# First MLP layer of two token blocks by Strassen-Winograd products, with folded weights kept in memory

## The chip, the core and the metric

The kernel runs on one core of a Trainium2 chip. A core has a matrix engine (TensorE, PE in the profile, with weight loads listed apart as PEld), a vector engine (DVE), a scalar engine (ACT), GpSimd (POOL), and SyncE (SP), which here only issues DMA transfers. Each engine works through its own queue of instructions in program order; semaphores tie the queues together. SBUF is the memory on the chip, with 128 partitions; PSUM is the memory that PE adds into, eight banks of 128x512 fp32. The metric is the device time of one execution in microseconds (us).

## The reference

x holds 2048 tokens of 640 features. xn is its layer norm. The output is x plus a linear attention of xn plus an MLP of xn with its own layer norm.

```python
xn = _layernorm(x, axis=-1)
return x + _A_ref(xn, A_wqkv, A_w_phi, A_wo) + _B_ref(xn, B_w1, B_b1, B_w2, B_b2)
...
qkv = (xn @ wqkv) -> q, k, v                          # 32 heads of 20
phi_q = [softmax(q @ w_phi), softmax(-q @ w_phi)]     # phi_k likewise
o = phi_q (phi_k^T v) / (phi_q phi_k^T 1), then @ wo
...
y = _layernorm(xn)
h = _gelu(y @ w1 + b1)                                # 640 -> 1728
return h @ w2 + b2                                    # 1728 -> 640
```

## The kernel before

**Arithmetic.** Every matmul of weight is done on fp32 operands that are split into a high and a low fp32r part. `split` (lines 50 to 60) does it: ACT copies the high part, and DVE or POOL subtracts it from the source for the low one. `mm3` (62 to 65) then runs three matmuls into the same bank, high by high, high by low and low by high; lines 63, 64 and 65 in the profile are these three. A product of 128 x 128 weights with 128 x 512 tokens is thus three matmuls of 128x512.

**Stages.** The 2048 tokens are four blocks of 512. Stage 1, up to about 225 us, runs the MLP of blocks 0 and 1 and, beside it, makes ready what the attention needs. Then come the projections to q, k and v (`proj`, for 16 tiles of 128 tokens and four banks of columns, which end at `CB` = 456, 908, 1362, 1856), the features and the k-v sums; then the MLP of blocks 2 and 3 beside the attention; then the output projection.

**The MLP in stage 1.** The 1728 hidden values are 14 chunks of 128; the last has 64. The five K chunks of 128 features make 15 matmuls for a chunk (`first`, line 242), after which `gelu` (249) has ACT read the bank, copy the high part, and DVE make the low part. Chunk 13 takes its high and low columns side by side, 10 matmuls, then an add on DVE and a subtraction on POOL (L278). A group g is two chunks. `passes(g, b, ws)` (253 to 295) is a generator: its first `next` runs the first layer of group g for block b, the rest the second layer, five output tiles m of 6 matmuls each (5 for the last group), each of which DVE adds into `acc[b]` (L293 with the bias for g = 0, L295 for the others). The second layer of one pass is run behind the first layer of the next. PSUM banks 0 to 2 (`ph`) are for the first layer, 3 and 4 (`px`) for work beside it, 5 to 7 (`po`) for the second layer: three outputs can stand before the first must be added.

**The work beside.** After every few matmuls the MLP steps a generator, `mlp.beside`. In most of stage 1 that is `prep` (478 to 531): it folds w_phi into the weights of k and q (L456, eight small matmuls and a split for the first part of each of 12 groups), takes statistics of blocks 2 and 3, splits the weights of v, transposes the statistics and sends them through memory (`rows`, 179, once for each block), and makes the normalised y of these blocks (L518, L521, L525, L528), stored to `y_dram`. The folded weights of k, v and the first of q stay in SBUF in `wkv_`; the other q weights go to `wq_dram` and are loaded at L573 for the projections.

**What sets the order.** PE's order is the program's throughout (`manual_schedule`, line 302). From line 351 to 558 (`order`) DVE, ACT and POOL keep the program's order too. A scheduler places the DMA issues on SP. After stage 1, L560 stores `acc` of the two blocks.

Of the kernel before, what the change touches and what calls it, by code (L numbers as in the profile page):

```python
# [15 lines left out]
P = 128  # L16
# [28 lines left out]
def tile_kernel(ctx: ExitStack, tc: tile.TileContext, x, xT, wkT, wqT, wv, wphi, wo, w1, b1, w2, b2,  # L45
# [24 lines left out]
    ones1 = cp.tile([1, P], F32, name="ones1")  # L70
# [11 lines left out]
    wq_dram = [tc.dram_tile([P, KC, CB[3] - CB[2]], F32, name=f"wq{p}") for p in "hl"]  # L82
    wo_dram = [tc.dram_tile([P, KC, D], F32, name=f"wo{p}") for p in "hl"]
    o_dram = [tc.dram_tile([2 * DH, 512], F32, name=f"o{b}") for b in range(NB)]
    r_dram = [tc.dram_tile([8, P], F32, name=f"r{b}") for b in range(NB)]
# [93 lines left out]
    def rows(b, xp, ptile):  # L179

        sc = xp.tile([P, 2, 4], F32, name="sc", bufs=1)
        nc.vector.tensor_copy(sc[:, 0, :], mv[:, 4 * b:4 * b + 4, 0])
        nc.vector.tensor_copy(sc[:, 1, :], ry[:, 4 * b:4 * b + 4])
        for _ in range(2):
            yield
        ps = ptile()
        nc.tensor.transpose(ps[:8, :P], sc.rearrange("p a t -> p (a t)"), idt)
        sr = xp.tile([8, P], F32, name="sr8", bufs=1)
        nc.vector.tensor_copy(sr, ps[:8, :P])
        nc.sync.dma_start(r_dram[b], sr)  # L190
        mr = mtile(5)
        nc.sync.dma_start(mr.rearrange("p a t -> p (a t)"),
                          r_dram[b].rearrange("r t -> (r t)").unsqueeze(0).to_broadcast([P, 8 * P]))
        return mr


    class Mlp:
        def __init__(self, slots, hid):
            self.hid, self.turn, self.slots, self.beside, self.raw = hid, 0, slots, iter(()), {}
            self.ph, self.px, self.po = Banks(0, 1, 2), Banks(3, 4), Banks(5, 6, 7)  # L200
# [14 lines left out]
        def take(self, c):  # L215
            w, parts = self.take_parts(c)
            for p in parts:
                p()
            return w

        def take_parts(self, c):

            r1, r2 = self.raw.pop(c)
            w = wp.tile([P, 4, D], F32R, name=f"w{self.slots[c % 4]}")
# [3 lines left out]
            def last():  # L228


                split(w1h[:, :, 0:64], w1h[:, :, 64:128], r1[:, :, 0:64])
                nc.vector.memset(f(w1l[:, :, 64:128]), 0.0)
                nc.vector.tensor_copy(w1l[:, :, 0:64], f(w1h[:, :, 0:64]))
                nc.scalar.activation(w2h, r2, AF.Copy)
                nc.vector.memset(f(w2l[64:128, :]), 0.0)
                nc.vector.tensor_tensor(w2l[0:64, :], r2[0:64, :], f(w2h[0:64, :]), op=ALU.subtract)

            return (w1h, w1l, w2h, w2l), [last] if c == 13 else [
# [14 lines left out]
        def passes(self, g, b, ws, hid=None):  # L253
# [7 lines left out]
            for j, (w1h, w1l, w2h, w2l) in enumerate(todo):  # L261
# [6 lines left out]
                else:  # L268
                    pz = self.ph()
                    for kc in range(KC):  # L270
                        nc.tensor.matmul(pz, w1h[:, kc, :], yh[:, kc, :], start=kc == 0, stop=False)
                        nc.tensor.matmul(pz, w1l[:, kc, :], yl[:, kc, :], start=False, stop=kc == KC - 1)
                    tm = gt[0:64, :]
# [6 lines left out]
            yield  # L280
            for m in range(KC):
# [12 lines left out]
                else:  # L294
                    nc.vector.tensor_tensor(acc[b][:, m, :], pw, acc[b][:, m, :], op=ALU.add)  # L295

# [42 lines left out]
    for c, pool in ((2, None), (3, r0)):  # L339
# [5 lines left out]
    for c in range(2, 4):  # L345
        dmas[c][1]()
    load_acc(0)
    for c in range(4):
        wc[c], parts[c] = mlp.take_parts(c)
# [33 lines left out]
    parts[2][0]()  # L383
# [5 lines left out]
    parts[3][0]()  # L389
# [26 lines left out]
    p10 = mlp.passes(1, 0, [wc[2], wc[3]])  # L416
    next(p10)
    finish(p00)
    for c in range(2, 4):
        parts[c][1]()  # L420
# [5 lines left out]
    mlp.fetch(4)  # L426

    wkv = ExitStack()
    kvw = wkv.enter_context(tc.tile_pool(name="wkv", bufs=1, side="right", reuse_waits="tile"))

    wkv_ = [kvw.tile([P, KC, CB[2]], F32R, name=f"wk{p}") for p in "hl"]
    rs = ExitStack()
    fp = rs.enter_context(tc.tile_pool(name="prep", bufs=2, side="right", reuse_waits="tile"))
    wpt = fp.tile([G6, 6, 6, DH], F32, name="wpt", bufs=1)
    nc.sync.dma_start(wpt, wphi)

    def raws(n, g):
        kk = G6 if g < 5 else 2 * DH
        raw = fp.tile([P, D], F32, name="raw")
        nc.sync.dma_start(raw[:kk, :], {"k": wkT, "q": wqT}[n][g * G6:g * G6 + kk, :])  # L440
        return raw

    def prep_fold(n, g, raw):
# [3 lines left out]
        if n == "k" or g == 0:  # L447
            c = slice(g * G5, g * G5 + kd) if n == "k" else slice(QK + D, CB[2])
            dst = [w[:, :, c] for w in wkv_]
        else:  # L450
            t = fp.tile([P, 2, KC, G5], F32R, name="t")[:, :, :, :kd]
            dst = [t[:, p] for p in range(2)]
        for k, ni in ((0, 4), (4, 1)):
# [4 lines left out]
            split(dst[0][:, k:k + ni], dst[1][:, k:k + ni], ps[:, :ni * kd].rearrange("p (i f) -> p i f", i=ni))  # L458
            for _ in range(3):
                yield  # L460
        if n == "q" and g:
            for p in range(2):
                nc.sync.dma_start(wq_dram[p][:, :, (g - 1) * G5:(g - 1) * G5 + kd], f(t[:, p]))

    def more_stats():

        for b in range(2, 4):
            def tiles():
                xbs = {}
                for t in (*range(4 * b, 4 * b + 4), None):  # L470
                    if t is not None:
                        xbs[t] = fp.tile([P, 2, KC, G5], F32, name="t").rearrange("p a c f -> p (a c f)")[:, :D]
                        nc.sync.dma_start(xbs[t], x[t * P:(t + 1) * P, :])
                    if xbs and t != 4 * b:
                        yield xbs.pop(min(xbs))
            yield from stats(range(4 * b, 4 * b + 4), fp, tiles())

    def prep():
        jobs = [(n, g) for n in "kq" for g in range(6)]
# [631 lines left out]
```

## Time and profile before

| | us |
|---|---|
| time, three runs | 737.65, 738.07, 739.62 (median 738.07) |
| profiled execution, span | 736.8 |
| first folding matmuls (L456) | 52.9 |
| first projection | 225.4 |

The profiled execution's own time is not given apart from its span; the median of the runs is 1.3 us above the span, which is what lies around it. In a row of the timeline stand the start, the duration, the engine, line, operation and its output and inputs, and in brackets how long the engine was idle before and what ended that. In a row of groups stand the count, the busy time, the mean in ns, and the idle time before.

### The profile page before, as it was taken

What the parts mean: (1) busy time and instruction counts of PE and PEld (TensorE: products, weight loads), DVE (VectorE), ACT (ScalarE), POOL (GpSimd) and SP (SyncE); (2) the same over time, 40 slices, a digit from 0 to 9 for tenths busy, and PEclk for the clock granted to TensorE, in tenths of its full rate; (3) what the DMA queues carried; (4) which work ended last, traced back from release to release, by engine and by line L of the source; (5) the groups of instructions that cost most, each with busy time, mean ns of one, the idle gap of its engine ahead of it and who ended that gap; (6) DMA issues with size and microseconds to landing.
All of it is one profiled execution on the core that took longest, in us unless ns stands there. A gap on an engine that the chain in (4) does not pass through costs nothing.

```text
span 736.8 us, 9681 instructions
## 1 busy us (share of the span) xinstructions
PE 723.8 (98%) x3441; PEld 610.2 (83%) x3441; DVE 479.9 (65%) x790; ACT 320.5 (44%) x526; POOL 370.6 (50%) x322
## 2 busy tenths in 40 slices
PE   9999999998999999999999999999999999999998
PEld 7788888777788998998998888888878888877886
DVE  7847645665653788788888788645575656767331
ACT  6624444332322464464345357256565556440110
POOL 2211222343321797797778889445586777304000
PEclk9999999999999999999999999999999999999999
DMA  9704477464543223633600706853433353153222
GB/s 317 221 19 141 143 177 178 141 193 142 159 161 144 75 86 144 161 101 150 143 0 1 179 1 200 196 149 107 126 116 114 113 157 90 48 215 127 83 84 73
DMA packets 64520, 95.36 MB, mean 129 GB/s; under 512 B 13312, under 2 KB 35216, under 8 KB 62848
## 3 DMA queue, kind: packets, MB, share of 16 engines
q1 hardware_dynamic: 64184, 94.74, 42.5%
q8 instruction: 27, 0.44, 0.3%
q14 instruction: 21, 0.17, 0.1%
q10 hardware_dynamic: 288, 0.01, 0.0%
HBM read 64.47 MB, written 30.26 MB: 129 GB/s over the span
## 4 chain that ended last, share of the span: by engine, by line
PE 73%; DVE 10%; DMA 5%; POOL 5%; ACT 3%; issue 3%; SPq 0%; POOLq 0%; DVEq 0%; ACTq 0%
PE bank L63 22%; PE bank L65 21%; PE bank L64 21%; PE bank L659 2%; PE bank L456 2%; POOL m L628 2%; PE bank L882 1%; DMA m<-r 1%; PE bank L881 1%; DVE acc L295 1%; DVE y L946 1%; DVE rx L925 1%; DVE m L57 1%; DMA raw<-in_wv 1%; DMA xb<-in_x 1%
## 5 line engine op out<-in xcount | busy, mean ns | idle before, releaser
L57 POOL TENSOR_TENSOR w<-r,w 128x640 fp32r<-128x640 f32 x52 | 83.2, 1618 | 107.6 <-ACT w L54 77.4
L63 PE MATMUL bank<-y,w 128*128 128x512 f32 (+1 forms) x334 | 131.1, 392 | 0.9 <-ACT m L250 0.6
L65 PE MATMUL bank<-y,w 128*128 128x512 f32 (+1 forms) x334 | 129.8, 389 | 0.3 <-POOL w L57 0.3
L64 PE MATMUL bank<-y,w 128*128 128x512 f32 (+1 forms) x334 | 129.6, 388 | 0.0
L63 PE MATMUL bank<-m,w 128*128 128x512 f32 x260 | 104.3, 401 | 4.6 <-DVE acc L295 3.8
L65 PE MATMUL bank<-m,w 128*128 128x512 f32 x260 | 101.8, 392 | 0.0
L64 PE MATMUL bank<-m,w 128*128 128x512 f32 x260 | 101.7, 391 | 0.0
L295 DVE TENSOR_TENSOR acc<-bank,acc 128x512 f32<-128x512 f32 x120 | 80.7, 682 | 16.7 <-PE bank L65 11.1
L57 DVE TENSOR_TENSOR m<-m,m 128x512 fp32r<-128x512 f32 (+1 forms) x54 | 45.0, 834 | 67.1 <-ACT m L54 67.1
L63 PE MATMUL bank<-wkh,y 128*128 128x456 f32 (+2 forms) x240 | 88.6, 369 | 0.0
L64 PE MATMUL bank<-wkl,y 128*128 128x456 f32 (+2 forms) x240 | 88.5, 369 | 0.0
L65 PE MATMUL bank<-wkh,y 128*128 128x456 f32 (+2 forms) x240 | 88.4, 368 | 0.0
L63 PEld LDWEIGHTS bank<-y,w 128*128 128x128 f32 x334 | 62.8, 188 | 14.1 <-DVE ob L1050 0.8
L65 PEld LDWEIGHTS bank<-y,w 128*128 128x128 f32 x334 | 62.7, 188 | 13.8 <-POOL w L57 0.7
L64 PEld LDWEIGHTS bank<-y,w 128*128 128x128 f32 x334 | 62.8, 188 | 12.7
L610 ACT ACTIVATE m<-bank 128x456 f32<-128x456 f32 (+3 forms) x64 | 27.0, 422 | 94.6 <-PE bank L65 78.2
L628 POOL TENSOR_TENSOR m<-m,mx 128x640 f32<-128x640 f32 (+2 forms) x48 | 44.5, 941 | 46.4 <-DVE mx L617 46.4
L63 PEld LDWEIGHTS bank<-m,w 128*128 128x128 f32 x260 | 48.9, 188 | 18.3 <-DVE acc L295 6.9
L875 POOL TENSOR_TENSOR e<-e,m 120x512 fp32r<-120x512 f32 (+1 forms) x28 | 38.1, 1362 | 43.2 <-ACT m L874 41.2
L65 PEld LDWEIGHTS bank<-m,w 128*128 128x128 f32 x260 | 48.8, 188 | 10.6
L631 DVE TENSOR_REDUCE sm<-m 128x64 f32<-128x1280 f32 x32 | 47.2, 1476 | 15.6 <-ACT m L629 15.5
L64 PEld LDWEIGHTS bank<-m,w 128*128 128x128 f32 x260 | 48.9, 188 | 9.6
(156 smaller groups left out, 1397.8 us busy)
## 6 DMA issues: line engine op xcount, KB each, us to landing
r<-in_w SPq DMA_DIRECT2D x52, 320.0 KB
e<-e SPq DMA_DIRECT2D x40, 240.0 KB
e<-acc SPq DMA_DIRECT2D x52, 160.0 KB
acc<-in_xT SPq DMA_DIRECT2D x4, 1280.0 KB
xb<-in_x SPq DMA_DIRECT2D x8, 320.0 KB
t<-in_x SPq DMA_DIRECT2D x8, 320.0 KB
raw<-in_xT SPq DMA_DIRECT2D x10, 256.0 KB
yh<-t SPq DMA_DIRECT2D x10, 256.0 KB
```

Of the source, the lines that this page charges most:

```text
L57: eng.tensor_tensor(lo, src, f(hi), op=ALU.subtract)
L63: nc.tensor.matmul(ps, lh, rh, start=first, stop=False, **kw)
L64: nc.tensor.matmul(ps, lh, rl, start=False, stop=False, **kw)
L65: nc.tensor.matmul(ps, ll, rh, start=False, stop=last, **kw)
L295: nc.vector.tensor_tensor(acc[b][:, m, :], pw, acc[b][:, m, :], op=ALU.add)
L456: nc.tensor.matmul(ps[:, i * kd:(i + 1) * kd], raw[:kk, (k + i) * P:(k + i + 1) * P], wpt[:kk, g, :kd // DF, 1:], start=True, stop=True)
L610: return nc.scalar.activation(p3[:, h:h + src.shape[1], 1:], src, AF.Copy).ins
L628: subs[n, t] = nc.gpsimd.tensor_tensor(ep[:, s], a, b, op=ALU.subtract)
L631: nc.vector.tensor_reduce(sm, e.rearrange("p s (h f) -> p (s h) f", f=DH), axis=AX, op=ALU.add)
L659: nc.tensor.matmul(kvp[g // 2][:VM, (g % 2) * 240:(g % 2) * 240 + 240].rearrange("p (s f) -> p s f", s=4), v[:, g * VS:g * VS + VM], ft[:, ...
L875: nc.gpsimd.tensor_tensor(pl, e, f(ph), op=ALU.subtract)
L881: nc.tensor.matmul(pn, kvs[:w, g, :], ph, start=True, stop=False)
```

## The change

**Order of the groups.** The start of stage 1 has groups 0 and 6 (chunks 0, 1, 12, 13) where it had groups 0 and 1. The splits of chunk 13 go to POOL there.

**Strassen-Winograd products.** Chunks 2 to 11, five pairs, run through the new `fast`, which takes both chunks of a pair and both blocks at once. On the first four K chunks (two by two) it makes seven products in place of eight, and the fifth K chunk is added plainly, one of its four products taken with a difference of weights (d5). That is 18 steps of `mm3`, 54 matmuls of 128x512, for 60. The weights are combined by `first_operands` (s1 to s4, d5, fifteen operations on POOL for a pair), the tokens once by `token_sums` (t1 to t4), which runs on POOL, DVE and ACT at the head of `mlp.beside`, ahead of `prep`. Three products are read out of PSUM by ACT, and three times DVE adds another to it. The second layer is cut out of `passes` as `second` and stepped between the products.

**Folded weights.** All folded weights, those of v too, are stored to `w_dram` and loaded into four banks before the projections (`load_bank`): bank 0 at the end of `prep`, into the tile that `prep` worked in; banks 1 and 2 into the tiles of the token sums; bank 3 into two weight slots. The low part of v is made in place, on POOL.

**Statistics.** The statistics of blocks 2 and 3 are finished, transposed once for both and sent through memory ahead of the weights of v. The buffers of v in the attention move to other tiles.

The core of the diff:

```diff
+        def second(self, g, b, hid, ws):
+
             for m in range(KC):
                 pw = self.po()
                 ms = slice(m * P, (m + 1) * P)
...
+        def fast(self, g, a, ts, hs, ms, more):
+
+            def product(ps, s, t, start=False):
+                for k in range(s[0].shape[1]):
+                    mm3(ps, s[0][:, k, :], s[1][:, k, :], t[0][:, k, :], t[1][:, k, :], start and k == 0, k == s[0].shape[1] - 1,
+                        skip_group_check=True)
+                    next(self.beside, None)
...
+            (b11, b21, b51), (b22, b52), (t1, t2, t3, t4) = ts
+            z1, z2, z3, gt = zs
+            pa = self.ph()
+            product(pa, a["11"], b11, True)
+            nc.scalar.activation(z1, pa, AF.Copy)
+            steps(1)
+            pc = self.ph()
+            product(pc, a["12"], b21, True)
+            product(pc, a["15"], b51)
+            nc.vector.tensor_tensor(z1, pc, z1, op=ALU.add)
+            h11 = hidden(0, z1, z1, hs[0])
+            steps(1)
+            product(pa, a["s2"], t2)
+            nc.scalar.activation(z2, pa, AF.Copy)
+            steps(1)
+            pd = self.ph()
+            product(pd, a["s1"], t1, True)
+            product(pd, a["25"], b52)
+            steps(2)
+            product(pa, a["s3"], t3)
+            nc.scalar.activation(z3, pa, AF.Copy)
+            nc.vector.tensor_tensor(z3, pd, z3, op=ALU.add)
+            h22 = hidden(1, z3, z3, hs[1])
+            steps(1)
+            product(pa, a["22"], t4)
+            product(pa, a["25"], b51)
+            h21 = hidden(1, pa, gt, hs[2])
+            steps(1)
+            product(pd, a["s4"], b22)
+            product(pd, a["d5"], b52)
+            nc.vector.tensor_tensor(z2, pd, z2, op=ALU.add)
+            h12 = hidden(0, z2, z2, hs[3])
+            steps(3)
+            return [[h11, h21], [h12, h22]]
...
-    p10 = mlp.passes(1, 0, [wc[2], wc[3]])
+    p10 = mlp.passes(6, 0, [wc[12], wc[13]])
...
+    def token_sums():
+
+        (h1, l1), (h2, l2) = y[0], y[1]
+        k1, k2 = slice(0, 2), slice(2, 4)
+        t1, t2, t3, t4 = tsum
...
+
+        r1, r2, r4 = more_z, mr3, mtile(5)
+        r3 = r1
+        yield from series(nc.gpsimd, r1, (h2[:, k1], ALU.subtract, h1[:, k1]), (None, ALU.add, l2[:, k1]), (None, ALU.subtract, l1[:, k1]))
+        yield from series(nc.vector, r2, (h2[:, k2], ALU.subtract, r1), (None, ALU.add, l2[:, k2]))
+        yield from part(t1, r1)
+        yield from series(nc.vector, r4, (h1[:, k2], ALU.subtract, r2), (None, ALU.add, l1[:, k2]))
+        yield from part(t2, r2)
+        yield from series(nc.gpsimd, r3, (h2[:, k2], ALU.subtract, h2[:, k1]), (None, ALU.add, l2[:, k2]), (None, ALU.subtract, l2[:, k1]))
+        yield from part(t4, r4)
+        yield from part(t3, r3)
...
+    def first_operands():
+
+        (a11, a12, a15), (a21, a22, a25) = [(r[:, 0:2, :], r[:, 2:4, :], r[:, 4:5, :]) for r in r1_]
+
+        def add(out, a, op, b):
...
+            split(*ops[n], src, eng=nc.gpsimd)
+
+        part("11", a11)
+        yield
+        part("12", a12)
+        part("15", a15)
+        yield
+        yield
+        s1, s2, s3, s4 = (sraw[:, i] for i in (0, 1, 0, 0))
+        add(s1, a21, ALU.add, a22)
+        part("s1", s1)
+        add(s2, s1, ALU.subtract, a11)
+        part("s2", s2)
+        yield
+        add(s3, a11, ALU.subtract, a21)
+        part("s3", s3)
+        yield
+        part("22", a22)
+        part("25", a25)
+        yield
+        add(s4, a12, ALU.subtract, s2)
+        part("s4", s4)
+        d5 = s2[:, 0:1]
+        add(d5, a15, ALU.subtract, a25)
+        part("d5", d5)
+        yield
...
+    def w_store(p, c0, src):
+        i = sum(c0 >= c for c in CB)
+        c0 -= CB[i - 1] if i else 0
+        nc.sync.dma_start(w_dram[i][p][:, :, c0:c0 + src.shape[2]], src)
...
+        finish(more)
+        mrs = [mtile(5), mr3]
+        yield from rows(fp, mlp.px, mrs)
...
+            hi = turn("t")[:, :D]
+            split(hi, raw.bitcast(F32R), raw, eng=nc.gpsimd)
+            for p, src in enumerate((f(hi), raw)):
+                for i, c0, c1 in ((1, 0, 300), (2, 300, D)):
+                    at = QK + c0 - CB[i - 1]
+                    nc.sync.dma_start(w_dram[i][p][:, kc, at:at + c1 - c0], src[:, c0:c1])
...
+        w = kvw.tile([P, 4560], F32R, name="pr")
+        load_bank(0, [[w[:, p * KC * CB[0]:(p + 1) * KC * CB[0]]] for p in range(2)])
+
+    def load_bank(i, places):
+
+        n = CB[i] - (CB[i - 1] if i else 0)
+        for p, pieces in enumerate(places):
...
+    mlp.beside = chain(token_sums(), prep())
+    ready = first_operands()
+    step(ready, 4)
+    p11 = mlp.passes(6, 1, [wc[12], wc[13]])
     next(p11)
+    step(ready, 3)
     finish(p01)
...
+    for s in range(1, 6):
+        if s == 2:
+            hm |= {0: mtile(0, F32R), 2: mtile(2, F32R)}
...
+        todo = [second_operands(s, r2)]
+        if s < 5:
+            load_first(s + 1)
+            todo.append(first_operands())
+        hid = mlp.fast(s, ops, tops, [hm[i] for i in used], ms, zip_longest(*todo))
+        finish(ms)
+        ws = [(None, None, *[mlp.tiles[2 * (s % 2 == 0) + j][:, 2 + p, :] for p in range(2)]) for j in range(2)]
+        ms = chain(*[mlp.second(s, b, hid[b], ws) for b in range(2)])
+        if s < 5:
...
     finish(mlp.beside)
-    finish(before)
+    r1b = kvw.tile([P, 2 * (CB[2] - CB[1])], F32R, name="r1b")
+    for i in range(2):
+        n = CB[i + 1] - CB[i]
+        most = kvw.tile([P, 4096], F32R, name=f"sums{i}")
+        load_bank(1 + i, [[most[:, 0:KC * n]], [most[:, KC * n:(2 * KC - 1) * n], r1b[:, 454 * i:454 * i + n]]])
+    load_bank(3, wq_)
+    finish(ms)
```

**Where instructions stand.** Three places are shown. First DVE, from the end of p10's second layer to the start of p01's; `m` are hidden values, `acc` the output sums of a block, `bank` PSUM. Before:

```order
L295 TENSOR_TENSOR acc_102<-bank_594,acc_102 128x512
L295 TENSOR_TENSOR acc_102<-bank_602,acc_102 128x512
L483 TENSOR_TENSOR wpt<-wpt 120x36x19
L57 TENSOR_TENSOR wkl<-bank_643,wkh 128x4x114
L57 TENSOR_TENSOR m_627<-m_626,m_627 128x512
```

Now (`y` are the parts of the tokens, `more_z` is r1, `mr_623` r2, `m_651` r4):

```order
L303 TENSOR_TENSOR acc_105<-bank_595,acc_105 128x512
L303 TENSOR_TENSOR acc_105<-bank_602,acc_105 128x512
L521 TENSOR_TENSOR mr_623<-y_149,more_z 128x1024
L521 TENSOR_TENSOR mr_623<-mr_623,y_150 128x1024
L57 TENSOR_TENSOR m_646<-m_645,m_646 128x512
L279 TENSOR_TENSOR m_645<-bank_673,m_645 64x512
L521 TENSOR_TENSOR m_651<-y_147,mr_623 128x1024
L521 TENSOR_TENSOR m_651<-m_651,y_148 128x1024
L301 SCALAR_TENSOR_TENSOR acc_106<-bank_704,b2t,acc_106 128x512
```

Four operations on 1024 columns have come in ahead of the first add of p01's second layer. On POOL, ahead of and behind them, stands now (`r` and `r1b` are raw weights, `w_175` to `w_178` the operands, `sraw` unsplit combinations, `sums` the token sums):

```order
L57 TENSOR_TENSOR w_176<-sraw,w_176 128x256
L560 TENSOR_TENSOR sraw<-sraw,r_627 128x256
L57 TENSOR_TENSOR w_176<-sraw,w_176 128x256
L521 TENSOR_TENSOR more_z<-y_149,y_147 128x1024
L521 TENSOR_TENSOR more_z<-more_z,y_150 128x1024
L521 TENSOR_TENSOR more_z<-more_z,y_148 128x1024
L527 TENSOR_TENSOR sums_614<-more_z,sums_614 128x1024
L282 TENSOR_TENSOR m_672<-m_645,m_672 64x512
```

Before, POOL had only the splits of whole chunks there. Second, ACT, at the start of `fast(1)`. Now:

```order
L54 ACTIVATE w_178<-sraw 128x256
L54 ACTIVATE w_178<-sraw 128x128
L525 ACTIVATE sums_614<-mr_623 128x1024
L525 ACTIVATE sums_615<-m_651 128x1024
L525 ACTIVATE sums_615<-more_z 128x1024
L328 ACTIVATE m_754<-bank_759 128x512
```

The copy L328 reads the first product out of its bank, and stands behind the copies of the operands and of three sums. Third, SP at the end of stage 1. Before:

```order
L573 DMA w_2013<-wqh 128x2470
L573 DMA w_2014<-wql 128x2470
L560 DMA a_89<-acc_102 128x2560
L560 DMA a_90<-acc_103 128x2560
L735 DMA woh<-r_2167 128x640
```

Now:

```order
L719 DMA w_1980<-wb3l 128x2470
L706 DMA yh_75<-pr 128x512
L706 DMA yl_76<-pr 128x512
L769 DMA a_92<-acc_105 128x2560
L719 DMA pr<-wb0h 128x2280
L719 DMA pr<-wb0l 128x2280
L769 DMA a_93<-acc_106 128x2560
```

The two loads of bank 0 have come in between the stores of the two blocks' sums.

More of the change, by code (lines that the diff above doesn't have):

```diff
@@ L1 @@
 from contextlib import ExitStack
-from itertools import zip_longest
+from itertools import chain, zip_longest
 import concourse.bass as bass
@@ L388, in tile_kernel @@
         centre(4 + i, x1[i])
-    parts[3][0]()
+    parts[13][0]()
     step(s47, 2)
@@ L437, in raws, with second_operands, one @@
+    def second_operands(s, r2):
+        def one(j):
+            split(*[mlp.tiles[2 * (s % 2 == 0) + j][:, 2 + p, :] for p in range(2)], r2, eng=nc.gpsimd)
+        yield
+        yield
+        one(0)
+        r2 = rp.tile([P, D], F32, name="r2")
+        nc.sync.dma_start(r2, w2[(2 * s + 1) * P:(2 * s + 2) * P, :])
+        yield
+        yield
+        yield
+        one(1)
+        yield
     def raws(n, g):
         kk = G6 if g < 5 else 2 * DH
-        raw = fp.tile([P, D], F32, name="raw")
+        raw = turn("raw")
@@ L511, in prep @@
         for b in range(2, 4):
-            mr = yield from rows(b, fp, mlp.px)
+            mr = mrs[b - 2]
             ahead = load(b, 0)
-            for _ in range(7):
+            for _ in range(3):
                 yield
```

228 lines of the change are left out of this document (134 added, 94 removed).

## The prediction

> **What bounds the kernel now.** The page's busy line and the table of TensorE's waits were read first, then the stretch of stage 1 behind its start, from 60 to 225 us; stage 1 is what the change rewrites.
>
> ```profile
> PE 723.8 (98%) x3441; PEld 610.2 (83%) x3441; DVE 479.9 (65%) x790; ACT 320.5 (44%) x526; POOL 370.6 (50%) x322
> PE bank L63 <- DVE acc L295: 3.8, 5, 1.6
> PE bank L187 <- DVE sc L183: 1.5, 2, 1.2
> 60.00:225.00 165.00, 160.21 (x743) 130.46 (x742) 100.14 (x182) 60.97 (x104) 48.70 (x34) 1.00 0.57 166
> ```
>
> TensorE (PE) is busy 98% of the 736.8 us span, and its dearest kind of wait is 3.8 us in all. In the stretch (the columns after the length are PE, weight loads, DVE, ACT, POOL, each with its instructions, then the granted clock, the DMA share and GB/s) PE is busy 160.2 of 165 us, and POOL 48.7. So in stage 1 a matmul that is removed shortens the run, and work on the other engines is free as long as PE never waits for it. The question is whether the added work on POOL, DVE and ACT always arrives in time.
>
> **What is removed.** The program has 1971 matmuls of 128x512 instead of 2001. Their pitch is read from two starts that lie 30 matmuls apart:
>
> ```profile
> 37.21 0.40 PE L63 MATMUL bank<-y,w 128*128 128x512 f32 x1
> 44.03 0.39 PE L63 MATMUL bank<-m,w 128*128 128x512 f32 x1
> ```
>
> 6.82 / 30 = 0.227 us, so 30 fewer are **-6.8 us**. This is the whole possible gain in arithmetic, under 1% of the time.
>
> **What is added at the start of the Strassen pairs.** Before `fast(1)` can run, POOL must make operands from the weights of chunks 2 and 3 (12, 15, s1, s2, then s3, 22, 25, s4, d5) and, with DVE and ACT, four sums over tokens (t1 to t4). No row before shows a two-tensor POOL operation of 128x1024, 128x256 or 128x128. The nearest rows are:
>
> ```profile
> L278 POOL TENSOR_TENSOR m<-m,m 64x512 fp32r<-64x512 f32 x4 | 5.2, 1292 | 36.1 <-ACT m L277 21.3 <-issue 14.8
> 9.10 1.56 POOL L57 TENSOR_TENSOR w<-r,w 128x640 fp32r<-128x640 f32 x1 [7.84 <-ACT w L54]
> L639 POOL TENSOR_TENSOR m<-m,w 128x1280 f32<-128x1280 f32 x16 | 38.0, 2372 | 3.6 <-DVE w L637 3.6
> L54 ACT ACTIVATE m<-m 128x512 fp32r<-128x512 f32 x50 | 31.6, 633 | 2.0 <-DVE acc L686 0.5
> L54 ACT ACTIVATE w<-m 128x1280 fp32r<-128x1280 f32 x16 | 20.4, 1277 | 6.0 <-POOL m L639 5.8 <-PE bank L663 0.2
> L54 ACT ACTIVATE m<-m 128x256 fp32r<-128x256 f32 x4 | 1.7, 419 | 0.1
> 186.69 0.69 DVE L57 TENSOR_TENSOR m<-m,m 128x512 fp32r<-128x512 f32 x1 [2.54 <-ACT m L54]
> 187.30 0.68 DVE L521 TENSOR_TENSOR raw<-raw,m 128x512 f32<-128x512 f32 x1
> L293 DVE SCALAR_TENSOR_TENSOR acc<-bank,b2t,acc 128x512 f32<-128x512 f32 x20 | 14.7, 736 | 3.6 <-PE bank L65 3.6
> ```
>
> POOL goes from 1.29 to 1.56 us for 128 columns more, 2.1 ns a column: an estimate of **2.35 us for 1024 columns**, 0.75 for 256 and 0.48 for 128. By L639, whose 1280 columns take 2.37 us (its second tensor is a small one, repeated), 1024 would be 1.9, the lower end; L57's 640 scaled up by 1.6 gives 2.5 to 2.6, the upper. I take 2.35, since L278 and L57 read two full tensors as the new lines do. ACT: between 512 and 1280 columns 0.84 ns a column, so 1.06 for 1024. DVE: two starts 0.61 apart for 512, so 1.2 for 1024.
>
> The chain begins when ACT has finished the hidden values of p01, whose copy is the first row below; POOL's and DVE's rows stand in program order, so what is late on one engine holds everything behind it.
>
> ```profile
> 44.96 0.63 ACT L54 ACTIVATE m<-m 128x512 fp32r<-128x512 f32 x1
> 52.88 1.04 PE L456 MATMUL bank<-wpt,raw 120*128 120x114 f32 x8
> 189.97 1.29 POOL L518 TENSOR_TENSOR raw<-raw,m 128x512 f32<-128x512 f32 x1 [3.14 <-DMA raw<-in_xT]
> 190.03 1.78 DVE L57 TENSOR_TENSOR m<-m,m 128x512 fp32r<-128x512 f32 x1 [2.05 <-ACT m L54]
> ```
>
> - First wait. From 45.6: POOL's operands before r1 (six of 256 columns, one of 128: 5.0, and three turns to ACT and back of 0.42: 1.3) end at about 52.0. r1 is three POOL operations, 7.05, and ends at **59.0**. DVE's r2 needs r1 and r4 needs r2; behind them in DVE's queue stands the first bias add of p01's second layer (now L301). So from 59.0: r2 2.4, a subtraction 0.6, chunk 13's add 0.6, r4 2.4, the add 0.74, together 6.8. A DVE operation that starts beside a POOL one lasts longer (189.97 and 190.03 above: 1.78 instead of 0.69, its end just one DVE operation after POOL's), and t1's lo runs on POOL just then, so I add one POOL operation, 2.35: **68.1**. PE, undisturbed, finishes p01's first layer at 44.0, then 25 matmuls (p10's second layer, 49.7), 25 (p11's first, 55.4) and 18 for m = 0 to 2 of p01's second layer: 59.5. For m = 3 it needs the bank that the held add empties. It waits **8.6 us** (6.3 without the held port).
> - Second wait. The product s2·t2 writes into the bank that z1 is read from (L328 on ACT), and L328 stands on ACT behind the hi copies of t2, t4 and t3; t3 comes from r3, last on POOL. From 68.1: POOL's chunk-13 subtraction (L282) until 68.7, five operations of 256 and three of 128 columns with their turns 6.3, t2's hi 1.06 and lo 2.35, r3 7.05, t3's hi 1.06, z1 0.6: **86.9**. Undisturbed PE stands there at 55.4 + 55 x 0.227 + 1.0 for a fold's eight matmuls (52.88) = 68.9. So both waits together are **18 us**, 9 of them in the second. Cost from below: with 1.9 us for 1024 columns and no turn waited for, r1 ends at 55.3 and s2·t2 is 6 us late; with the turns, 9. From above, at 2.6 and with DVE and POOL holding each other up twice more, 24.
>
> **PE after a wait.** Behind a wait of that length PE may run slowly at first.
>
> ```profile
> 1.31 6.60 PE L364 MATMUL bank<-m 128*128 128x512 f32 x18 [1.31 <-POOL m L362]
> 0.00:2.00 2.00, 0.69 (x2) 0.59 (x3) 0.17 (x1) 0.82 (x1) 0.73 (x5) 1.00 0.18 23
> 178.79 0.50 PE L63 MATMUL bank<-m,w 128*128 128x512 f32 x1 [1.63 <-DVE acc L295]
> ```
>
> The 18 matmuls at the start of the run took 6.6 us where 18 x 0.227 is 4.1: 2.5 us lost, although the granted clock reads 1.00. The longest wait in mid-kernel, 1.63 us, is followed at once by the usual pitch. The new waits are longer than that, though a fold's small matmuls may fall into them. I take one loss of 2.5, between none and three (7.5). [...]
>
> **Other terms of the pairs.** In `fast(1)` only p11's five steps of second layer lie between the products, so the turn from one product to the next in the same bank (a copy of 0.6 and the semaphores) is partly uncovered: **+1**, between 0 and 3. In the later pairs ten steps stand there, and POOL's work per pair (15 operations, 9, and two splits of 1.6) fits into about 26 us of PE; cost nothing. If that cover fails, it is a further rival.
>
> **The loads before the projections.** All folded weights now go to memory and back. Bank 0 is loaded behind the store of block 0's result on SP's queue.
>
> ```profile
> 220.64 0.32 SPq L560 DMA_DIRECT2D a<-acc  x1
> 225.39 0.36 PE L63 MATMUL bank<-wkh,y 128*128 128x456 f32 x1
> a<-acc SPq DMA_DIRECT2D x2, 1280.0 KB
> 212.00:214.00 2.00, 2.00 (x10) 1.67 (x9) 0.57 (x1) 1.32 (x2) 0.00 (x0) 1.00 1.06 443
> 222.00:224.00 2.00, 2.00 (x10) 1.68 (x9) 1.37 (x2) 0.00 (x0) 0.00 (x0) 1.00 0.99 410
> ```
>
> That store waits for the last add of block 0, issued 4.75 us before the first projection. With block 1's last 30 matmuls in place of 25 it is 5.9 before. Store and loads move 1.31 + 2 x 1.17 = 3.64 MB; with the DMA share at 1, 410 to 443 GB/s were moved, so 8.7 us, from 5.3 before the projection (0.6 after the add, two issues of 0.32) to 3.4 after, and 0.8 to land: **+4.2**. Ends: 2.7 (443, and landing at once) to 6. Banks 1 to 3 are not behind that store.
>
> The rest of the added traffic (banks 0 to 2 stored and loaded, 7 MB each way, on 41 more issues of 0.32 us on SP) spreads over stage 1, where 14 MB in 165 us are 85 GB/s beside the 166 moved there at a share of 0.57: by that share 0.86, still below 1. Cost nothing; if the banks 1 to 3 came late, PE would wait at the second projection, which is the last rival's kind.
>
> **Gaps that go.** From 60 to 225 us PE idles 165 - 160.2 = 4.8 us, most of it the two kinds of waits quoted first: late adds (L295) and the statistics' transposition (L187), which now happens once for both blocks, earlier. Some of it will stay, since adds can still be late: **-2**, between -4.8 and +4 (v now splits on POOL, whose queue is longer, and its stores go behind that).
>
> **The sum.** -6.8 + 18.0 + 2.5 + 1 + 4.2 - 2 = +16.9. It is made on the profiled execution, span 736.8 and 1.3 around it up to the median of 738.07, which is in its middle; so **755.0**.
>
> **Rivals.**
> - Shorter waits: POOL's lower price, or turns that overlap, and no held port. A delay of 6 to 11 with one loss or none, + 1 + 4.2 - 2 - 6.8: +2.4 to +9.9, 741 to 748. For it speaks L639; against it that its second operand is small.
> - The clock: each of three waits costs 2.5 instead of one, +5: 760, with longer ends 759 to 765. The start of the run speaks for it; that the 1.63 us wait was followed by the full pitch, against.
> - Not slower: POOL's chain up to r1 and r3 is covered. [...] Against it: three dependent POOL operations stand there behind seven others.
> - Further stalls: the steps of `prep` are put off by the sums, and what is left at the end runs with PE idle; over 765. POOL's 6 to 12 us in 28 speak against.
> - That the change does not save what it says is excluded: the order has 30 matmuls fewer.
>
> **How the numbers follow.** Forecast, 748 to 759: 0.48. Shorter waits, 741 to 748: 0.17. Clock, 759 to 765: 0.15. Not slower, up to 740.3: 0.12. Over 765: 0.08. The range 741 to 765 holds the first three, 0.80. A measurement of this kernel tells about 0.3% (2.2 us) from no change; faster, below 735.9, takes 0.07 of the fourth case, the same 0.05, slower 0.88.
>
> **What the profile after would show.** A gap of PE between about 59 and 68 us that DVE's bias add of `acc` ends; a second at 78 to 87 that ACT's z1 (L328) ends, behind the copies of L525; a gap at the first projection that the DMA of bank 0 ends; thirty matmuls fewer at L63 to L65, POOL's busy time up. Wrong would be: r1 on POOL done before 55.5; no gap of over 2 us between 55 and 90; the first projection without a wait; or slow matmuls behind each gap (the clock) or behind none.

## The result and the profile after

| | before | after |
|---|---|---|
| median time, us | 737.96 (737.65 to 739.62, 4 runs) | 797.65 (795.32 to 798.75, 4 runs) |
| profiled span, us | 736.8 | 793.5 |
| first projection starts, us | 225.4 | 278.0 |

The change made the kernel slower: ratio 1.0795, interval 1.0775 to 1.0816. The forecast of 755.0 (741.0 to 765.0) had the sign and missed the size. The first lines of the page of after, and its row of granted clocks in 40 slices:

```profile
span 793.5 us, 9866 instructions
PE 735.3 (93%) x3410; PEld 615.6 (78%) x3410; DVE 490.3 (62%) x796; ACT 343.5 (43%) x587; POOL 441.7 (56%) x411
PEclk9997998998899999999999999999999999999999
```

There are 31 matmuls fewer (30 of them the saved ones), and yet PE is busy 11.5 us longer; the granted clock, full throughout before (mean 1.000), has four slices at 7 or 8 from the fourth to the eleventh (mean 0.972). Of the 56.7 us between the two profiled spans, 52.6 lie ahead of the first projection. (The medians lie 59.7 us apart: the profiled execution of after took 795.32 us and is the fastest of its four, so its trace shows some 2.3 us less than the median run lost.) The table of PE's waits in after (total, times, longest):

```profile
PE bank L63 <- DVE acc L303: 11.9, 5, 5.7
PE bank L63 <- DVE acc L301: 10.2, 2, 8.6
PE bank L625 <- DVE pr L57: 8.7, 3, 6.1
PE bank L63 <- DVE more_z L345: 4.8, 1, 4.8
PE bank L63 <- ACT more_z L344: 4.1, 3, 2.6
PE bank L63 <- ACT m L328: 3.3, 1, 3.3
PE bank L64 <- DMA pr<-wb0l: 3.0, 1, 3.0
PE bank L625 <- issue: 2.5, 1, 2.5
```

Two kinds had cost PE 5.3 us before; these eight cost 48.5. The pitch, below, is the time from the start of one matmul to the start of the next. Taken apart by the timeline of PE, the 56.7 us are:

| term | forecast, us | measured, us |
|---|---|---|
| 30 matmuls fewer | -6.8 | -6.8 |
| waits at the start of the products (L301 8.6, a fold behind the sums 2.5, L328 3.3) | 18.0 | 14.3, and 3.7 of slow matmuls between them |
| slow matmuls behind waits, beyond those 3.7 | 2.5 | 11.7 |
| read-outs of PSUM in the pairs (L344) | 1 | 4.1 |
| bank 0 | 4.2 | 5.0 |
| waits behind loads and stores of `prep`, and behind POOL's operands, in the pairs | 0 | 24.2 |
| old gaps | -2 | -2.7 net |
| longer pitch of matmuls | 0 | 2.5 |
| sum | +16.9 | +56.0 |

"Slow matmuls" are starts that come more than 0.1 us later than the full pitch behind a 128x512 matmul, idle time taken off: 18.1 us in all from 20 us to the first projection, against 2.7 before. The old gaps were 5.3 us from 20 us on; 2.6 of waits at 27 and 34 us stand in their place, so -2.7. The longer pitch is 0.2310 against 0.2279 us (means over 575 and 666 successive matmuls at full clock), times some 830.

The product s2·t2 started at 88.34 us; the working had 86.9:

```profile
69.05 0.80 PE L63 MATMUL bank<-m,w 128*128 128x512 f32 x1 [8.58 <-DVE acc L301]
88.34 0.49 PE L63 MATMUL bank<-sums,w 128*128 128x512 f32 x1 [3.25 <-ACT m L328]
L521 POOL TENSOR_TENSOR more_z<-more_z,y 128x1024 f32<-128x1024 f32 x4 | 9.5, 2387 | 0.3
```

The estimated 2.35 us for 1024 columns on POOL measured 2.39, and the first wait 8.58 for 8.6. What the working calls a held port is a DVE operation that lasts longer beside one of POOL: the second of r2, beside t1's low part on POOL, took 3.29 us, the first 1.22 and the two of r4 1.20 and 1.23. No run shows a port. What was missing comes behind that. In the timeline of DVE, at PE's two largest waits between the start and 135 us:

```profile
102.35 0.89 DVE L130 BATCH_NORM_STATS2 st<-m 128x6 f32<-128x320 f32 x2 [5.01 <-DMA m<-in_x]
106.32 0.64 DVE L345 TENSOR_TENSOR more_z<-bank,more_z 128x512 f32<-128x512 f32 x1
129.13 0.89 DVE L130 BATCH_NORM_STATS2 st<-mr 128x6 f32<-128x320 f32 x2 [5.47 <-DMA mr<-in_x]
130.18 0.64 DVE L333 TENSOR_TENSOR m<-bank,m 128x512 f32<-128x512 f32 x1
132.87 0.27 DVE L57 TENSOR_TENSOR pr<-bank,pr 128x114 fp32r<-128x114 f32 x1
```

DVE stands on the load of an x tile for the statistics, and what PE waits for is behind it in the same queue. At 107 us that is the add that empties PE's bank (L345). At 133 us the way is longer: from L333 over ACT's gelu and its copy of a fold to DVE's low part of that fold (the last row), which PE's next folding matmuls need. PE's own rows name DVE, and only DVE's name the load. In before, DVE's waits for x tiles between 50 and 226 us were these (total, times, longest):

```profile
DVE st L129 <- DMA t<-in_x: 1.5, 2, 1.2
```

While DVE stood there in after, the transfers were full (the last two numbers are the DMA share and GB/s; 1.18 shows that the share of so short a stretch is rough):

```profile
96.00:100.00 4.00, 3.30 (x19) 2.53 (x19) 1.30 (x4) 1.76 (x4) 2.95 (x5) 1.00 1.00 132
100.00:104.00 4.00, 2.25 (x11) 1.54 (x9) 1.61 (x5) 0.00 (x0) 0.17 (x1) 1.00 1.01 317
124.00:128.00 4.00, 3.09 (x17) 2.29 (x16) 0.00 (x0) 0.00 (x0) 0.00 (x0) 1.00 1.18 151
```

The two loads were issued at 96.04 and 121.53 us, among stores of folded weights, and DVE went on 6.3 and 7.6 us later. The same holds for ACT and the weights of v, at 190 to 198 us:

```profile
189.94 0.74 ACT L54 ACTIVATE pr<-pr 128x640 fp32r<-128x640 f32 x1 [3.21 <-DMA pr<-in_wv]
195.07 0.74 ACT L54 ACTIVATE pr<-pr 128x640 fp32r<-128x640 f32 x1 [3.26 <-DMA wb1l<-pr]
195.72 0.71 ACT L252 ACTIVATE m<-m,b1t 128x512 f32<-128x512 f32 x1
197.12 0.85 DVE L57 TENSOR_TENSOR more_m<-m,more_m 128x512 fp32r<-128x512 f32 x1 [8.25 <-ACT more_m L54]
```

The second of them waits for a store: ACT wrote this buffer again only when its store to `wb1l` had landed, 3.26 us on. Behind it stands the gelu of a hidden tile (L252), behind that DVE, behind DVE the adds of `acc` (L303) for which PE waited 5.70 us. The wait of 1.86 us at 188 us came by the same way from the load before, on which ACT had stood 1.29 us. At v the transfers were not full: the share was 0.70 from 188 to 192 us and 0.89 from 192 to 196.

### The profile page after: what moved, and what is told of

Same layout as the page of the kernel before. It is cut to its first block, busy times and chain, and to the rows that moved or that the text cites. A ratio compares the mean times of both kernels' runs of the same rounds, so it can differ in the third digit from the quotient of the medians.

```text
span 793.5 us, 9866 instructions
## 1 busy us (share of the span) xinstructions
PE 735.3 (93%) x3410; PEld 615.6 (78%) x3410; DVE 490.3 (62%) x796; ACT 343.5 (43%) x587; POOL 441.7 (56%) x411
## 2 busy tenths in 40 slices
DMA packets 77738, 109.33 MB, mean 138 GB/s; under 512 B 22944, under 2 KB 47664, under 8 KB 75552
## 4 chain that ended last, share of the span: by engine, by line
PE 64%; POOL 11%; DVE 8%; DMA 6%; issue 6%; ACT 4%; SPq 0%; POOLq 0%; ACTq 0%; DVEq 0%
PE bank L63 19%; PE bank L65 19%; PE bank L64 19%; POOL w L57 3%; POOL m L835 2%; POOL more_z L521 2%; PE bank L866 2%; POOL sraw L560 1%; DMA pr<-wb0l 1%; PE bank L1089 1%; PE bank L1088 1%; DMA pr<-in_xT 1%; DVE st L130 1%; DMA mr<-in_x 1%; PE bank L625 1%
## 5 line engine op out<-in xcount | busy, mean ns | idle before, releaser
L63 PE MATMUL bank<-y,w 128*128 128x512 f32 (+1 forms) x284 | 113.4, 399 | 5.3 <-DVE more_z L345 4.8
L64 PE MATMUL bank<-y,w 128*128 128x512 f32 (+1 forms) x284 | 112.0, 394 | 0.0
L65 PE MATMUL bank<-y,w 128*128 128x512 f32 (+1 forms) x284 | 112.0, 394 | 0.0
L57 POOL TENSOR_TENSOR w<-r,w 128x640 fp32r<-128x640 f32 (+3 forms) x58 | 78.7, 1370 | 59.4 <-ACT w L54 42.9
L63 PE MATMUL bank<-m,w 128*128 128x512 f32 x220 | 90.2, 410 | 22.3 <-DVE acc L303 11.9
L303 DVE TENSOR_TENSOR acc<-bank,acc 128x512 f32<-128x512 f32 x120 | 80.7, 681 | 14.6 <-PE bank L65 10.2
L64 PE MATMUL bank<-m,w 128*128 128x512 f32 x220 | 88.0, 400 | 0.9 <-DVE m L57 0.9
L65 PE MATMUL bank<-m,w 128*128 128x512 f32 x220 | 88.3, 401 | 0.0
L63 PEld LDWEIGHTS bank<-m,w 128*128 128x128 f32 x220 | 42.3, 192 | 35.0 <-DVE acc L303 15.1
L63 PEld LDWEIGHTS bank<-y,w 128*128 128x128 f32 x284 | 54.7, 193 | 17.0 <-DVE more_z L345 5.2
L65 PEld LDWEIGHTS bank<-y,w 128*128 128x128 f32 x284 | 54.7, 192 | 11.7
L64 PEld LDWEIGHTS bank<-y,w 128*128 128x128 f32 x284 | 54.8, 193 | 11.2
L57 DVE TENSOR_TENSOR m<-m,m 128x512 fp32r<-128x512 f32 (+1 forms) x41 | 33.9, 826 | 43.5 <-ACT m L54 43.4
L63 PE MATMUL bank<-sums,y 128*128 128x454 f32 (+1 forms) x160 | 59.4, 371 | 0.0
L65 PE MATMUL bank<-sums,y 128*128 128x454 f32 (+1 forms) x160 | 58.9, 368 | 0.0
L836 ACT ACTIVATE m<-m,rs_all 128x1280 f32<-128x1280 f32 x32 | 43.7, 1366 | 22.6 <-POOL m L835 22.6
L1098 ACT ACTIVATE ts<-bank 64x512 f32<-64x512 f32 (+1 forms) x44 | 26.1, 593 | 56.0 <-PE bank L1089 50.8
L64 PEld LDWEIGHTS bank<-m,w 128*128 128x128 f32 x220 | 42.5, 193 | 9.9 <-DVE m L57 1.5
```

Of the source, the lines that this page charges most:

```text
L57: eng.tensor_tensor(lo, src, f(hi), op=ALU.subtract)
L63: nc.tensor.matmul(ps, lh, rh, start=first, stop=False, **kw)
L64: nc.tensor.matmul(ps, lh, rl, start=False, stop=False, **kw)
L65: nc.tensor.matmul(ps, ll, rh, start=False, stop=last, **kw)
L836: exps[n, t] = nc.scalar.activation(e, e, AF.Exp, scale=rs_all[:, t:t + 1])
L1098: nc.scalar.activation(t, pn[z, :], AF.Copy)
```

## Experiments

Theory A: loads and stores of `prep` are late, and DVE, ACT and POOL hold PE up behind them. Theory B: the products' own operands, sums and read-outs overload the queues. Theory C: PE runs slowly after having been idle.

**Everything but the products.** Chunks 2 to 11 with `passes`, `mlp.beside = prep()`:

```diff
-    mlp.beside = chain(token_sums(), prep())
+    mlp.beside = prep()
...
-    for s in range(1, 6):
...
-        hid = mlp.fast(s, ops, tops, ...)
...
+    for g in range(1, 6):
+        for b in range(2):
+            this = mlp.passes(g, b, ws)
```

> Everything of the change except the Strassen products: chunks 2 to 11 run as plain first layers (30 matmuls more than after), without token sums and operands; folded weights still go through memory, statistics still come first. Theory A (the added stores crowd the transfers, so the loads of x, v weights and xT land late, and DVE, ACT and POOL stand on them in program order while PE's adds wait behind): the waits behind those loads stay, 755 to 775. Theory B (the operands, sums and PSUM read-outs of the products are too much for the queues, and the loads are only late because the queues are): 740 to 746, that is 738 and a wait of some 5 us for bank 0.

779.46 us, one run. That is 41.6 us above before with no product in it, even above A's range. Between 60 and 97 us PE's waits are again behind x tiles and folds:

```profile
69.16 0.89 DVE L130 BATCH_NORM_STATS2 st<-m 128x6 f32<-128x320 f32 x2 [3.24 <-DMA m<-in_x]
71.51 0.50 PE L63 MATMUL bank<-m,w 128*128 128x512 f32 x1 [3.49 <-DVE acc L301]
95.31 0.89 DVE L130 BATCH_NORM_STATS2 st<-mr 128x6 f32<-128x320 f32 x2 [4.93 <-DMA mr<-in_x]
PE bank L63 <- ACT w L54: 12.8, 1, 12.8
```

It is not a clean yardstick for the size. The last row's 12.8 us wait is the one behind the weights of v, larger than in after: ACT stood on their loads for 10.89, 1.20 and 5.96 us. Another of 8.6 us is of this kernel only: the tiles of the sums are free here, so loads of banks 1 and 2 went out on SP from 162 us on, and POOL stood 13.19 us on a load of xT issued among them.

**Without the stores.**

```diff
     def w_store(p, c0, src):
-        nc.sync.dma_start(w_dram[i][p][:, :, c0:c0 + src.shape[2]], src)
+        pass
...
-            for p, src in enumerate((f(hi), raw)):
-                for i, c0, c1 in ((1, 0, 300), (2, 300, D)):
...
-                nc.sync.dma_start(f(w), w_dram[i][p][:, at:at + m])
+                nc.sync.dma_start(f(w), w_dram[3][p][:, at:at + m, 0:n])
```

> After, with all stores of folded and v weights left out; the banks are loaded from two pieces of y that are stored once, early (so the attention's weights are wrong). Theory A: the waits at 107, 120 to 133, 188 and 198 us shrink to under 1 us each, some 20 us of idle time and 8 of slow matmuls: 765 to 775. Theory B: they stay, 790 to 798.

782.31 us, one run: 15.3 less than after's median (13.0 less than its profiled execution), and 7 short of A's range. The waits at 107 and 133 fell from 4.77 to 1.48 and from 6.11 to 1.84, the two on L303 near 190 from 1.86 + 5.70 to one of 3.08; of the two at folds from 120 to 124, one grew from 1.62 to 2.60 and the other stayed. The windows from 88 to 140 us, of after and then of this kernel (the last two numbers are the DMA share and GB/s):

```profile
88.00:140.00 52.00, 37.50 (x169) 30.06 (x170) 25.93 (x69) 22.91 (x49) 20.63 (x24) 0.90 0.75 159
88.00:140.00 52.00, 43.67 (x192) 34.84 (x193) 27.55 (x72) 24.73 (x53) 22.43 (x27) 0.87 0.36 108
```

The stores added 51 GB/s and 0.39 of share there, far more share for a byte than the loads. They make the loads late, though not alone.

**Without most x loads.**

```diff
-                    if t < 4 * b + 4:
+                    if t < 10:
                         nc.sync.dma_start(places[t % 2], x[t * P:(t + 1) * P, :])
```

> After, with six of the eight loads of x tiles for the statistics of blocks 2 and 3 left out (statistics of the wrong tokens). Theory A: DVE no longer stands on these loads at 102 and 129 us; PE's waits at 107 (4.8) and 120 to 133 (8.7 in three) go with some 4 us of slow matmuls: 778 to 784. Theory B: 794 to 798.

783.03 us, one run: 14.6 less than after's median, 12.3 less than its profiled execution. The waits at 107 and 133 are gone (10.9 us) and slow matmuls fell from 18.1 to 14.2 us. Some of it was lost again at later waits: the one on L328 grew from 3.25 to 4.86 and the larger one behind v from 5.70 to 6.95. The two smaller waits at folds stayed (2.57 and 1.12 us), so those are not the x loads'. In both the fold's copy stands on ACT behind the copy of an operand, which waits in the first for POOL (1.44 us) and in the second for a load of the next weights (2.01 us); in after it is the same.

**PE kept busy in the first wait.**

```diff
+                if (g, b, m) == (0, 1, 3):
+                    pd = self.px()
+                    for _ in range(36):
+                        nc.tensor.matmul(pd, ws[0][2][:, 0:P], hid[0][0], start=True, stop=True)
```

> After, with 36 matmuls of 128x512 into an unused bank ahead of the fourth output tile of p01's second layer, where PE waited 8.6 us; their result is not used. If PE is slow behind a wait because it was idle (theory C), the slow matmuls from 69 to 73 us go, 2.1 us: 793 to 796, and the granted clock of 60 to 72 us reads 1.00. If the slow stretch has another cause: 797 to 799, with the same low clock.

798.35 us, one run: no gain. The windows of PE of after, then twice of this kernel (length, PE's busy time, granted clock, DMA share, GB/s):

```profile
60.00:72.00 12.00, 3.42 (x10) 0.62 0.00 0
60.00:72.00 12.00, 11.48 (x51) 1.00 0.00 0
84.00:96.00 12.00, 7.91 (x30) 0.64 0.28 76
```

The first wait shrank to 0.52 us and the clock there read 1.00, as C has it. But the second wait grew from 3.25 to 7.62 us, s2·t2 started at 88.09, and the slow matmuls came behind that (0.64 in the third row). The start's end is set by POOL and ACT, and PE's slowness ahead of it is hidden: what the clock gave back in the first wait was waited away in the second.

**The token sums on DVE.**

```diff
-        yield from series(nc.gpsimd, r1, ...
+        yield from series(nc.vector, r1, ...
-        yield from series(nc.gpsimd, r3, ...
+        yield from series(nc.vector, r3, ...
```

> After, with the six operations of r1 and r3 on DVE instead of POOL, nothing else changed. If the start's delay is POOL's chain, as the prediction worked it out, the wait of 8.6 us on L301 falls below 3, the one on L328 goes, and s2·t2 starts at 70 to 73 us instead of 88.3: 778 to 784. If the delay sits elsewhere (loads of the weights, ACT), s2·t2 stays beyond 80 and the time above 790.

786.3 us (784.98 to 787.61, 2 runs), ratio to before 1.0654 (1.0631 to 1.0676), 11.4 less than after, and above the 778 to 784 expected. The wait on L301 fell to 4.11 us, not below 3, that on L328 to 0.18, and s2·t2 started at 77.7: later than expected, and 10.6 earlier than in after. So r1 and r3 on POOL are 10.6 of the 19.4 us by which s2·t2 was late. The other 8.8 stay with the sums on DVE, whose own chain still holds L301 up, and with slow matmuls behind that wait.

**Bank 0 in larger pieces.** The same bytes, with a layout by fold:

```diff
+    w_dram[0] = [tc.dram_tile([P, 4, KC, G5], F32, name=f"wb0{p}") for p in "hl"]
...
+        if i == 0:
+            nc.sync.dma_start(w_dram[0][p][:, c0 // G5], src)
```

> After, with bank 0 laid out in memory so that each partition's row of a stored fold is one piece of 2280 bytes instead of five of 456; the same bytes. If the stores crowd the transfers by their number of small pieces, the waits at 107 and 120 to 133 shrink by half or more: 786 to 792. If only their bytes count, or the loads are late for another reason: 796 to 799.

793.95 us (793.11 to 794.79, 2 runs), 3.7 less, between the two expectations. The packets under 512 bytes fell from 22944 to 17824, the waits at 107 and 133 from 4.77 to 2.00 and from 6.11 to 3.09. The first says little, since the run with bank 0 ahead of the sums, below, has 2.21 there with the small pieces. At the other wait, four runs that keep the small pieces (the two above and the next two) have 4.58 to 5.85, so there the number of pieces is a part of it.

**Three buffers for v.**

```diff
-            raw = turn("raw")
+            raw = (*raw_, f(pr[:, 3560:4200]))[kc % 3]
...
-        ahead = load_v(0)
+        ahead = [load_v(0), load_v(1)]
...
```

> After, with three buffers in place of two for the weights of v, loaded two ahead. If the wait of 5.7 us at 198 (and 1.9 at 188) comes from a load that may only start when the stores of the buffer before have landed, it falls below 2 us, with 2 to 3 us of slow matmuls: 787 to 792. If the transfers are simply full there, it stays: 796 to 799.

798.83 us (796.77 to 800.88, 2 runs): no gain, but not because the transfers are full. ACT now waits for the other pair of buffers, which takes the high part, and there for the landing of stores as well (2.06 and 2.96 us, the rows below); PE's wait is 5.71 us. At the next pair PE waits 7.33 us for another reason: POOL stands 10.17 us on a load of xT, and L328 behind POOL's operands.

```profile
187.80 0.74 ACT L54 ACTIVATE pr<-pr 128x640 fp32r<-128x640 f32 x1 [2.06 <-DMA wb2h<-pr]
192.64 0.74 ACT L54 ACTIVATE pr<-pr 128x640 fp32r<-128x640 f32 x1 [2.96 <-DMA wb2h<-pr]
```

**Bank 0 ahead of the stores of the sums.**

```diff
+                loads[i] = nc.sync.dma_start(f(w), w_dram[i][p][:, at:at + m])
...
+    with tc.issue_after(loads[0].ins):
         for b in range(2):
             nc.sync.dma_start(a_dram[b], acc[b])
```

> After, with the stores of both blocks' sums issued behind the loads of bank 0 instead of before and after them. By the prediction's own step the 1.31 MB ahead of bank 0 cost 3 us of the 5 us wait at the first projections: 793 to 795. If bank 0 waits for prep's last stores: 796 to 798.

794.17 us (793.68 to 794.98, 4 runs), 3.5 less. But the waits for bank 0 fell only from 4.98 to 3.44 us, and the profiled execution (794.98) is just 0.3 us below that of after (795.32); the wait at 107 happened to be 2.21 in it, which the edit does not touch. So the trace shows 1.5 us for the place of the store, not 3, and leaves the rest of the 3.5 open. The store now goes out right behind the loads and moves beside them, so what its bytes cost is not shown apart.

**The causes together.** DVE's sums, no stores, no x loads, each by the edit shown:

> After, with r1 and r3 on DVE, without the stores of folded and v weights, and without six of the eight loads of x tiles (attention weights and statistics wrong). If the three causes measured alone add up: 797.7 - 11.4 - 15.3 - some 8 that the x loads still cost without stores = 763, 757 to 768. If something else stands behind the waits: over 775.

763.80 us (763.13 to 764.46, 2 runs), ratio 1.0341 (1.0319 to 1.0363), inside the range that follows if the three add up. That range takes only 8 us, an estimate, for the x loads: the three measured alone come to 41.3 us, and together they gave 33.9, since stores and x loads stand behind the same waits. What is left above before has two of the eight x loads and none of these stores in it, but still the start (4.09), v and xT (3.08, 2.29), bank 0 (5.3) and slow matmuls (11.0 us).

**The products alone.** Both kernels without `prep`, the one of after with DVE's sums:

```diff
     def prep():
-        nc.sync.dma_start(wpt, wphi)
...
+        for b in range(2):
+            for p in range(2):
+                nc.sync.dma_start(y_dram[b][p], f(y[b][p]))
+        nc.vector.tensor_copy(rs_all[:, 8:16], rs_all[:, 0:8])
```

> After with r1 and r3 on DVE and with all of prep left out (no folding, no statistics and y of blocks 2 and 3, no weights of v; the attention reads pieces of y instead); against before with the same left out. The products alone: 30 matmuls fewer (-6.8), some 5 us of start (a wait of 4.1 in the run with DVE's sums, and slow matmuls) and 1 to 3 us for read-outs of PSUM: 0 to 3 us faster than before without prep. If the products' read-outs are the trouble: more than 5 us slower than it.

> Before, with the same left out of stage 1: the yardstick for the run above. Its 13 small matmul groups of folding and most of its 4.8 us of gaps go: 720 to 728.

728.91 us (727.53 to 729.60, 4 runs) with the products, 717.35 (717.05 to 717.62, 4 runs) without: 11.6 slower, neither kernel having `prep`, where 0 to 3 us faster was expected. The windows from 60 to 95 us, with and without the products:

```profile
60.00:95.00 35.00, 25.95 (x95) 20.31 (x94) 20.24 (x23) 14.63 (x28) 27.99 (x23) 0.85 0.09 29
60.00:95.00 35.00, 35.00 (x156) 28.96 (x156) 14.16 (x20) 11.32 (x18) 12.43 (x8) 1.00 0.43 140
```

Here PE loses 9.1 us idle (5.72 on L301 and 3.33 on L344) and 4.5 in slow matmuls; the rest of stage 1 has no wait of over 0.3 us. With -6.8, and 2.4 us of longer pitch (0.2305 for 0.2267), that is 9.2 of the 10.6 us between the two starts of the projections. So the start alone cost 13.6 us here, where some 5 were expected, even with r1 and r3 on DVE. The later pairs run without waits, as forecast, when nothing is loaded beside them; their longer pitch was not forecast.

**Three corrections that compute everything.** DVE's sums, bank 0 in larger pieces, and bank 0 first:

> After, with three corrections that compute everything: r1 and r3 on DVE, bank 0 in pieces of 2280 bytes, bank 0's loads ahead of the stores of the sums. Added up: 797.7 - 11.4 - 3.7 - 3.5 = 779, 776 to 782. If the corrections free time that the next wait takes: 784 to 790.

779.18 us (776.83 to 779.91, 4 runs), ratio 1.0544 (1.0524 to 1.0564): they add up, and it is still far slower than before. No version that beats before was found.

## Why the prediction was wrong

- **Right:** the saved matmuls, 6.8 us; the mechanism and place of the start's delay (18 us forecast, s2·t2 19.4 us behind its undisturbed 68.9); bank 0's wait (4.2 forecast, 5.0 measured), in part by luck. The store and the loads took 11.7 us (269.8 to 281.5) where the working had 9.5, at 326 and 358 GB/s with the share near 1 (272 to 280 us) and not at 410 to 443; but they began 6.3 us ahead and not 5.3. The 0.8 us to land in that sum stands in no run here.
- **The step that failed** is in the part on the loads: the rest of the added traffic "spreads over stage 1 ... by that share 0.86, still below 1. Cost nothing". The amount came out as worked out: 0.86 over 165 us is 142 us at full share, and the measured mean of 0.67 from 60 to 278 us is 146. But it did not spread evenly, and waits that were put at nothing cost 24.2 us. Of these 18.5 are behind loads and stores that landed late: 10.9 behind x tiles, where the share stood at 1.00 to 1.18, and 7.6 behind v, where the share was lower (0.70 and 0.89) and ACT stood 3.26 us on the store of a buffer that it was to write. Another 1.0 is behind a load of the next weights, and 3.1 lie among the steps with xT at the end, of which 2.3 are the same in the run without the stores. At the mean share of 0.67 the bytes fitted, but single loads did not land in time for the in-order queues that waited for them (5.01 and 5.47 us on x tiles), and `prep` loads just one piece ahead. The part on the pairs called POOL's work covered, at nothing; read-outs and a fold that stand behind POOL's operands waited 5.7 us (the 4.1 of the table, and 1.6 of the 24.2).
- **Gaps that go, -2**, had a bound of +4, on account of v on POOL. That bound came from today's waits, and did not count the waits of ACT for a store to land, nor x tiles.
- **One loss of 2.5 behind a wait** was mis-sized. Of nine waits of 1.86 us or more between 60 and 270 us, eight were followed by slow matmuls, which came to 15.4 us more than before in all. The rival on the clock, at 0.15, had the mechanism (with PE kept busy in the first wait, the granted clock of 60 to 72 us read 1.00 and not 0.62), but priced three waits. A row of before spoke against it, a wait of 1.63 us with no loss behind; that was true, but did not decide: in after one of 1.66 us had no loss behind it either, and one of 1.86 us had. In after the clock read 0.50 from 64 to 72 us, slow matmuls started 0.43 us apart for 0.23, and the slow stretch behind the wait of 1.86 us lasted 3.4 us (189.15 to 192.53).
- **Further stalls, over 765**, was the case that came, at 0.08. Its mechanism as written, that the work of `prep` is put off to the end, did not occur.
- Left open: how much of the lateness is the number of pieces, the landing of stores, or SP's order (without the stores 6.4 of these 18.5 us stayed), and why the pitch is longer. That the x loads were late because the transfers were full fits the share at that moment and the runs without stores and without x loads, but no run parts it from their place on SP; in before the share also stood at 1.09 and 1.05 from 108 to 116 us, and no wait of DVE for an x tile was over 1.2.

## What to carry to other kernels

Before counting added transfers as free, list the instructions that wait for each load or for a buffer's store to land, and what stands behind them in the same in-order queue; a mean share of the DMA engines below 1 says nothing on that (here 0.67, with 18.5 us of waits behind late loads and stores), so look at the share stretch by stretch. When arithmetic saves 1% on an engine that is 98% busy, every new wait of 2 us on that engine can cost nearly 4 (here 1.86, and 1.7 of slow matmuls behind it), so the saving must be set against the number of new dependences and not only against work.

## What the runs showed of the hardware

A wait of 1.66 us (at 34.07) was followed by matmuls at the full pitch. Behind one of 1.86 the next three starts follow after 0.34, 0.23 and 0.26 us, and then come eight after 0.39 to 0.43, up to PE's next wait (some of the rows):

```profile
188.32 0.50 PE L63 MATMUL bank<-m,w 128*128 128x512 f32 x1 [1.86 <-DVE acc L303]
189.15 0.63 PE L63 MATMUL bank<-m,w 128*128 128x512 f32 x1
189.58 0.63 PE L64 MATMUL bank<-m,w 128*128 128x512 f32 x1
192.14 0.56 PE L64 MATMUL bank<-y,w 128*128 128x512 f32 x1
192.53 0.39 PE L65 MATMUL bank<-y,w 128*128 128x512 f32 x1
```

So one such stretch costs some 1.7 us, and begins 0.8 us after the wait. The length of the wait alone does not decide: the one of 3.25 us at 88.34 was followed by the full pitch, and the same wait of 3.29 us, in the run with bank 0 loaded first, by slow matmuls; and in that run 1.78 us were enough (1.6 us of slow matmuls behind it). Further, matmuls that read the token sums had a mean pitch of 0.233 to 0.236 us, and those that read `more_m` 0.232 to 0.235, where those that read `y` had 0.229 to 0.230, in the same run of after and at full clock; no run here shows why.
